# Rows of y scattered into a table in the experts' order, in a dense block followed by a routed one

## The chip, the cores and the metric

One NeuronCore of one Trainium2 chip runs the kernel. The metric is device time in microseconds (us): the median over runs of one launch. TensorE is called PE in the profile, VectorE DVE, ScalarE ACT, GpSimd POOL, and SyncE SP. SP issues most DMAs here; POOL issues the indirect ones, in which a list of 128 numbers says which rows of a table in DRAM are read or written.

## The reference

Three stages follow one another on 4608 tokens (8 batches of 576) of width 512.

```python
kv = np.einsum('bhsd,bhse->bhde', k, v)              # linear attention, 8 heads of 64
out = np.einsum('bhsd,bhde->bhse', q, kv)
x = out / np.sqrt(np.mean(out * out, -1) + 1e-6) * g_norm
h = x @ w_in                                         # dense block, 512 -> 2048 -> 512
y = (np.maximum(h, 0) + alpha * np.minimum(h, 0)) @ w_out
e_idx = np.argmax(y @ w_gate, axis=1)                # 8 experts, one for each token
gate_w = softmax(y @ w_gate)[e_idx];  eom = sigmoid(y @ w_output_gate)[e_idx]
out[mask] = gate_w * eom * (np.maximum(y[mask] @ w1[e], 0) @ w2[e])   # 512 -> 1024 -> 512
```

## The kernel before

**The dense stage** takes the tokens in 12 blocks of 384 (`NBLK`), each of three tiles of 128. For every block PE makes 16 pieces of h, then three tiles of y. The steps that follow a tile of y (`y_tail`) write it, scaled, as a pair of 16-bit floats into an SBUF tile `row` (ACT line L663, then a VectorE step), transpose it by an SP DMA into `yT` (L668) and multiply it with the gate weights (`l`, L681). `route_1` and `route_2` then find each token's expert and its place among the expert's tokens; the place, as a row number, is `pos` (L728). Beside this, small steps of the attention of later blocks run on all engines (`qs`, `rs` and `x` on POOL, `qT` transposes on SP, `ops` on PE).

**What the routing leaves in DRAM.** Two tables are written in each block. `lst` is a list of token numbers by expert, of 4 bytes an entry: POOL scatters 128 of them for each tile of a block, 36 scatters in all (L731). `ytab` holds the rows of y by token, 2052 bytes each (1024 16-bit values and one scale): SP writes them with plain DMAs (L760 and L764). `lst` is filled at the start with a number out of range (`dmy`, L1193, 8 DMAs), so that empty places of a list are skipped later.

**The expert stage** works in 38 slots of 128 tokens (and two that are skipped unless the data need them): four `s` slots of the fullest expert, run while the last dense block is still being routed, 31 `d` slots and three pairs `p` of half slots, each with one expert's weights. The `d` slots are dealt to four lanes of weights (`lane0` to `lane3`, 4 MB each, loaded by SP in 1 MB pieces when the expert of a lane changes). `tables` and `unit_tables` work out on DVE, after the last block's routing, which expert and which stretch of its list each slot has, as `tabi` and `utabi`.

For each slot the engines do this, in a written order for PE and SP: SP reads the slot's start out of `tabi` into a register and loads 128 entries of `lst` (`load_list`, L1038 and L1039); POOL gathers those rows of `ytab` into `yg` (L882); SP transposes them to `byT` (L891); PE makes `bh` (L1088) with a lane; ACT and DVE turn it into `h`; SP transposes it to `hT` (L1097); PE makes `bo` (L1110); ACT scales it; and POOL scatters it to the output by the same list (L1114). Three gather buffers (`NYG`) and five transposed ones (`NYT`) let the rows run ahead; the order in which SP issues all this is fixed when the program is built, and SP issues in order: a DMA that waits holds up those behind it.

These lines decide which gathers may be issued when (`l` counts the lists loaded, `x` the slots transposed, `t` the slots that PE has finished with, `g` the gathers):

```python
def rows_ahead():
    ...
    while done["g"] < min(done["l"], done["t"] + NYT, done["x"] + NYG, done["end"]):
        gather(done["g"])
```

Of the kernel before, what the change touches and what calls it, by code (L numbers as in the profile page):

```python
# [20 lines left out]
P = 128  # L21
# [11 lines left out]
TB = 3  # L33
# [15 lines left out]
UNITS = 2 * (len(PAIRS) + RARE)  # L49
SLOTS = FULL + len(PAIRS) + RARE  # L50
RT = 48
NLIST = E * RT * P
DUMMY = 1 << 20
ROW = DM + 1
# [10 lines left out]
def body(ctx: ExitStack, tc, q, k, v, g_norm, w_in, w_out, alpha, w_gate, w_og, w1, w2, out):  # L65
# [5 lines left out]

    ytab = dram.tile([NT, ROW], I32, name="ytab")
    lst = dram.tile([NLIST, 1], I32, name="lst")
    lsts = dram_disjoint_views(lst, TB)
    outs = dram_disjoint_views(out, SLOTS)
    ws = dram.tile([E, P, WCOLS], F16, name="ws")
# [21 lines left out]
    dve.tensor_scalar(out=base0, in0=iota_f, scalar1=float(RT * P), scalar2=None, op0=ALU.mult)  # L98
# [6 lines left out]
    for G in range(B // 2):  # L105
        for half in range(2):
            b = 2 * G + half
            pool.iota(ids[:, 9 * G + 4 * half:9 * G + 4 * half + 4], pattern=[[1, 4]], base=b * S,
                      channel_multiplier=4)
            pool.iota(ids[64 * half:64 * half + 64, 9 * G + 8:9 * G + 9], pattern=[[1, 1]],  # L110
                      base=b * S + 512, channel_multiplier=1)
    mhalf = const.tile([P, E], F32, name="mhalf")
# [63 lines left out]
    tp, yp = left("tp", 2), left("yp", 3)  # L176
    rawp, stg, cv = right("rawp", 5), right("stg", 2), right("cv", 2)
    kvp, qp, at = right("kvp", 2), right("qp", 2), right("at", 2)

    gts = [gpool.tile([P, 2, GF, BLK], F16, name=f"g{j}") for j in range(NG)]  # L180
# [471 lines left out]
    def y_tail(i, u, ps, lg, ys, rows, wait=5):  # L652
# [8 lines left out]
        rowt = yp.tile([P, ROW], I32, tag="row", name="row" + nm)  # L661
# [49 lines left out]
    def route_2(i, lg, ys, rows, oh, oh16, se):  # L711
# [23 lines left out]
        scatter(0)  # L735
        for u in range(1, TB):
            if i < NBLK - 2:
                side.extend([lambda: None] * 2 + [partial(scatter, u)])
            else:
                scatter(u)  # L740

# [11 lines left out]
        for u in range(TB):  # L753
            dve.tensor_tensor(out=rows[u][:, DM:ROW].bitcast(F32), in0=rc[:, 0, u:u + 1], in1=ys[:, u:u + 1],
                              op=ALU.mult)
            G, t = divmod(i * TB + u, 9)
            if t < 8:
                b = 2 * G + t // 4
                dst = ytab[b * S:b * S + 512, :].rearrange("(p j) c -> p j c", j=QJ)[:, t % 4, :]
                sp.dma_start(out=dst, in_=rows[u])  # L760
            else:
                for half in range(2):
                    r0 = (2 * G + half) * S + 512
                    sp.dma_start(out=ytab[r0:r0 + 64, :], in_=rows[u][64 * half:64 * half + 64, :])  # L764
# [14 lines left out]
    AHEAD, NYG, NYT = 7, 3, 5  # L779
# [4 lines left out]
    def star():  # L784
# [18 lines left out]
        dve.tensor_scalar(out=si[:, 1:2], in0=si[:, 0:1], scalar1=float(RT), scalar2=None, op0=ALU.mult)  # L803
        dve.tensor_copy(out=star_i, in_=si)
        with sp_after():
            e = sp.value_load(star_i[0:1, 0:1], min_val=0, max_val=E - 1)
            t0 = sp.value_load(star_i[0:1, 1:2], min_val=0, max_val=(E - 1) * RT)
            lv = lst.rearrange("(t p) o -> t p o", p=P)
            for j in range(STAR):
                t = bp.tile([P, 1], I32, tag="idx", name=f"idx_s{j}", bufs=10)  # L810
                i = sp.dma_start(out=t, in_=lv[bass.ds(t0 + j, 1)].rearrange("t p o -> (t p) o"))
                jobs.append(dict(nm=f"s{j}", lanes=[0], idx=t, k=kst))
            done["l"] = STAR
# [12 lines left out]
    done = dict(t=0, g=0, x=0, l=0, end=SLOTS - RARE)  # L826

    def rows_ahead():
# [3 lines left out]
        while done["g"] < min(done["l"], done["t"] + NYT, done["x"] + NYG, done["end"]):  # L832
# [27 lines left out]
    def after(x):  # L860
# [3 lines left out]
        if (layer, n) == (2, 0):  # L864
            lists(STAR + 4)
        if layer == 1 and n >= STAR - 1:
            lists(min(done["end"], n + AHEAD))
# [8 lines left out]
    def lists(end):  # L876
        while done["l"] < end:
            load_list(done["l"])
            done["l"] += 1

    def gather(n):
        pool.indirect_dma_start(out=ygs[n % NYG], out_offset=None, in_=ytab,  # L882
                                in_offset=bass.IndirectOffsetOnAxis(ap=jobs[n]["idx"][:, 0:1], axis=0),
                                bounds_check=NT - 1, oob_is_err=False)

    def turn(n):
# [7 lines left out]
        pool.tensor_tensor(out=j["msc"], in0=yg[:, DM:ROW].bitcast(F32), in1=j["k"], op=ALU.mult)  # L894
# [30 lines left out]

    def slot_k(ohs, nm):
# [6 lines left out]
    def unit_tables(es_d):  # L933
# [385 lines left out]
```

## Time and profile before

| | |
|---|---|
| median of 3 runs | 1438.72 us (1436.63 to 1442.8) |
| the profiled execution | 1453.03 us, of which 1451.3 us are its span |
| granted TensorE clock, mean of the span | 0.943 of full speed |
| PE busy | 1298.0 us, 89% of the span |
| DVE, ACT, POOL busy | 835.9, 563.2 and 327.6 us |

The profiled execution is 1.0% above the median of the timed runs. The stages lie in the span like this: the attention of the first block, the weights' conversion and the first dense block until about 320 us, the other dense blocks to about 985, the four `s` slots with the last block's routing to about 1040, then the `d` and `p` slots to 1436.9.

### The profile page before, as it was taken

To read this page: it belongs to the slowest core of one execution; us is meant where nothing else is said; L and a number is where in the kernel's file an instruction comes from. 1 tells how busy PE (TensorE), PEld (TensorE's weight loads), DVE (VectorE), ACT (ScalarE), POOL (GpSimd) and SP (SyncE) were. 2 spreads that over 40 slices of the span, in tenths; PEclk is the share of its full clock that TensorE was granted. 3 is DMA by queue.
4 is the path that set the end of the run, shared out by engine and by line. 5 is a ranking of instruction groups with operands and counts; after the bars stand their busy time and mean duration, and the time that the engine had idled before them with its cause. 6 is when DMAs were issued, how large, how long until landed. Compare 5 with 4: busy or idle time off the path is not lost. (4 is left out here: it accounts for less than half of the span.)

```text
span 1451.3 us, 22236 instructions
## 1 busy us (share of the span) xinstructions
PE 1298.0 (89%) x7586; PEld 667.3 (46%) x7586; DVE 835.9 (58%) x2470; ACT 563.2 (39%) x928; POOL 327.6 (23%) x320
## 2 busy tenths in 40 slices
PE   4679995798999989999999999999688999699996
PEld 3435542454555545555455555554233443244442
DVE  5899777568787867778696877445111211121220
ACT  3355553346555535556555655321011111011111
POOL 2023334132213332212222212011212121121211
PEclk8579997899999989999999999999899999899998
DMA  9944046757594947785846665149897888889751
GB/s 260 268 117 143 3 119 143 74 119 228 118 279 109 245 124 162 201 211 180 183 108 154 178 162 147 23 120 167 238 245 185 167 194 218 196 189 226 164 118 37
DMA packets 336628, 236.71 MB, mean 163 GB/s; under 512 B 257260, under 2 KB 290044, under 8 KB 332032
## 3 DMA queue, kind: packets, MB, share of 16 engines
q1 hardware_dynamic: 320064, 199.56, 59.4%
q0 software_dynamic: 7232, 18.92, 4.4%
q10 hardware_dynamic: 9216, 16.78, 3.5%
q8 instruction: 61, 1.00, 0.3%
q14 instruction: 55, 0.45, 0.1%
HBM read 248.07 MB, written 53.19 MB: 208 GB/s over the span
## 5 line engine op out<-in xcount | busy, mean ns | idle before, releaser
L586 PE MATMUL h<-x,wi 128*128 128x384 f16 x2304 | 419.6, 334 | 9.9 <-DMA x<-x 5.8
L605 PE MATMUL y<-wo,g 128*128 128x512 f16 x1728 | 409.7, 384 | 12.5 <-ACT g L593 7.3
L586 PEld LDWEIGHTS <-wi 128*128 128x128 f16 x2304 | 225.5, 100 | 171.8 <-issue 21.4
L605 PEld LDWEIGHTS <-g 128*128 128x128 f16 x1728 | 165.3, 98 | 198.2 <-issue 11.0
L1094 DVE CAST h_d<-br_d 128x512 f16<-128x512 f32 x62 | 26.7, 431 | 296.9 <-DMA hT_d<-h_d 187.4
L1088 PE MATMUL bh_d<-lane,byT_d 128*128 128x512 f16 x744 | 168.6, 383 | 8.4 <-DMA lane<-ws 8.4
L1110 PE MATMUL bo_d<-lane,hT_d 128*128 128x512 f16 x744 | 168.9, 384 | 7.9 <-DMA hT_d<-h_d 7.9
L593 ACT CAST g<-r 128x384 f16<-128x384 f32 x192 | 97.5, 510 | 133.0 <-DVE r L591 127.8
L591 DVE SCALAR_TENSOR_TENSOR r<-m,alphat 128x384 f32<-128x384 f32 x192 | 123.1, 642 | 24.8 <-ACT m L589 23.3
L1088 PEld LDWEIGHTS <-byT_d 128*128 128x128 f16 x744 | 73.2, 99 | 99.5 <-issue 14.6
L1110 PEld LDWEIGHTS <-hT_d 128*128 128x128 f16 x744 | 72.8, 99 | 100.1 <-DMA hT_d<-h_d 11.2
L334 POOL TENSOR_TENSOR rs<-ms,mhalf 128x8 f32<-128x8 f32 x36 | 67.6, 1879 | 225.8 <-DVE qm L337 209.7
L589 ACT ACTIVATE m<-h,scal 128x384 f32<-128x384 f32 x160 | 91.7, 575 | 39.4 <-PE h L586 36.5
L594 DVE TENSOR_TENSOR g<-r,g 128x384 f16<-128x384 f32 x160 | 93.1, 583 | 23.8 <-ACT g L593 21.4
L396 DVE SCALAR_TENSOR_TENSOR wlo_w<-rawe,es_w,whi_w 128x1024 f16<-128x1024 f32 x64 | 85.4, 1350 | 25.9 <-ACT whi_w L395 14.6
L1092 ACT ACTIVATE br_d<-bh_d 128x512 f32<-128x512 f32 x62 | 37.0, 598 | 144.9 <-PE bh_d L1088 121.1
L526 ACT ACTIVATE eab_w<-rawe 128x1024 bf16<-128x1024 f32 x64 | 67.2, 1057 | 58.7 <-DMA rawe<-in_moe_w_dram 52.2
L395 ACT ACTIVATE whi_w<-rawe,es_w 128x1024 f16<-128x1024 f32 x64 | 71.3, 1144 | 40.3 <-DMA ws<-whi_w 19.1
L1113 ACT ACTIVATE ob_d<-bo_d,msc_d 128x512 f32<-128x512 f32 x31 | 21.3, 687 | 142.3 <-PE bo_d L1110 142.3
L731 POOL DMA_INDIRECT lst<-ids,pos x36 | 37.3, 1036 | 171.9 <-DVE pos L728 109.2
L357 POOL TENSOR_TENSOR x<-xs,x 128x512 f16<-128x512 f32 x30 | 46.6, 1552 | 113.4 <-ACT x L356 84.4
L882 POOL DMA_INDIRECT yg<-ytab,idx_d x31 | 32.7, 1053 | 154.5 <-DMA idx_d<-lst 96.0
(341 smaller groups left out, 1353.9 us busy)
## 6 DMA issues: line engine op xcount, KB each, us to landing
lane<-ws SPq DMA_DIRECT2D x150, 1024.0 KB
rawe<-in_moe_w_dram SPq DMA_DIRECT2D x64, 512.0 KB
ws<-whi_w ACTq DMA_DIRECT2D x64, 256.0 KB
ws<-wlo_w SPq DMA_DIRECT2D x64, 256.0 KB
ytab<-row SPq DMA_DIRECT2D x32, 256.5 KB
q<-in_q_dram SPq DMA_DIRECT2D x16, 512.0 KB
rawwi<-in_moe_w_in_dram SPq DMA_DIRECT2D x16, 512.0 KB
rawwo<-in_moe_w_out_dram SPq DMA_DIRECT2D x16, 512.0 KB
```

The lines of the kernel that those rows point to most:

```text
L334: pool.tensor_tensor(out=rs, in0=ms, in1=mhalf, op=ALU.pow)
L395: act.activation(out=dst_h, in_=src, func=AF.Copy, scale=s)
L396: dve.scalar_tensor_tensor(out=dst_l, in0=src, scalar=s, in1=dst_h, op0=ALU.mult, op1=ALU.subtract)
L526: act.activation(out=ab.rearrange("p a b -> p (a b)"), in_=raws[4 * m + i], func=AF.Abs)
L586: pe.matmul(ps, wi[:, f // 4 * NC + c, w, fs], xt[i][:, xc, :], start=(n == 0), stop=(n == 3 * NC - 1))
L589: act.activation(out=r0, in_=ps, func=AF.Copy, scale=(scst if start else scal)[:, f:f + 1])
L591: dve.scalar_tensor_tensor(out=r, in0=r0, scalar=alphat[:, f:f + 1], in1=r0, op0=ALU.mult, op1=ALU.max)
L593: act.copy(out=hi, in_=r)
L594: (pool if start else dve).tensor_tensor(out=lo, in0=r, in1=hi, op=ALU.subtract)
L605: pe.matmul(ps, g[:, t, f % GF, us], wo[:, f, w, :], start=(start and m == 0), stop=(stop and m == 2))
L1088: pe.matmul(hp[ts], j["yT"][:, x, ts], w1_[:, w, c, hs], start=(m == 0), stop=(m == 3 * NC - 1))
L1110: pe.matmul(po[ts], hT[:, g, ts], w2_[:, w, f, :], start=(m == 0), stop=(m == 3 * NFE - 1))
```

## The change

The token lists go. In the changed kernel `ytab` has a row for every place of every expert (8 times 4608), and the row that is scattered carries the token's number: its width grows from 513 to 528 words (2112 bytes), with the scale in word 512 and the token in word 513. POOL copies the token numbers into the row tile (L758) and scatters the whole tile to `pos` (L761), so SP's plain writes of rows and POOL's scatters of lists are both replaced by one indirect DMA a tile. The row tiles are three fixed ones rather than a pool of buffers, and in blocks 0 to 9 the scatters have the whole `ytab` as their target, in blocks 10 and 11 separate views of it. A slot's row numbers follow from its table entry by arithmetic on DVE (`slot_rows`, a few operations for all `d` slots and a few for the `p` slots), so SP loads no lists; the output's row numbers come with the gathered rows (`oidx`, L890). The lines of the later functions shift: the `yT` transposes are L682, the gathers L876, `byT` L885, the lanes' loads L1059, `hT` L1094 and the output L1111.

```diff
         pos = small.tile([P, TB], I32, tag="pos", name="pos" + nm)
         dve.tensor_copy(out=pos, in_=pf)
 
-        def scatter(u):
-            pool.indirect_dma_start(out=lsts[u], out_offset=bass.IndirectOffsetOnAxis(ap=pos[:, u:u + 1], axis=0),
-                                    in_=ids[:, i * TB + u:i * TB + u + 1], in_offset=None, bounds_check=NLIST - 1,
-                                    oob_is_err=False)
...
         for u in range(TB):
-            dve.tensor_tensor(out=rows[u][:, DM:ROW].bitcast(F32), in0=rc[:, 0, u:u + 1], in1=ys[:, u:u + 1],
+            dve.tensor_tensor(out=rows[u][:, DM:DM + 1].bitcast(F32), in0=rc[:, 0, u:u + 1], in1=ys[:, u:u + 1],
                               op=ALU.mult)
...
-                sp.dma_start(out=dst, in_=rows[u])
+            pool.tensor_copy(out=rows[u][:, DM + 1:DM + 2], in_=ids[:, i * TB + u:i * TB + u + 1])
+
+        def scatter(u):
+            pool.indirect_dma_start(out=ytabs[u] if i >= NBLK - 2 else ytab, out_offset=bass.IndirectOffsetOnAxis(ap=pos[:, u:u + 1], axis=0),
+                                    in_=rows[u], in_offset=None, bounds_check=NLIST - 1, oob_is_err=False)
...
-        while done["g"] < min(done["l"], done["t"] + NYT, done["x"] + NYG, done["end"]):
+        while done["g"] < min(len(jobs), done["t"] + NYT, done["x"] + NYG, done["end"]):
...
-                                in_offset=bass.IndirectOffsetOnAxis(ap=jobs[n]["idx"][:, 0:1], axis=0),
-                                bounds_check=NT - 1, oob_is_err=False)
+                                in_offset=bass.IndirectOffsetOnAxis(ap=jobs[n]["row"], axis=0),
+                                bounds_check=NLIST - 1, oob_is_err=False)
...
+        j["idx"] = small.tile([P, 1], I32, tag="oidx", name="oidx_" + j["nm"], bufs=NYT + 3)
+        pool.tensor_tensor(out=j["idx"], in0=yg[:, DM + 1:DM + 2], in1=j["pad"], op=ALU.add)
...
+        at = slotp.tile([P, n], F32, name="at" + nm)
+        dve.tensor_scalar(out=at, in0=st, scalar1=float(w), scalar2=col, op0=ALU.mult, op1=ALU.add)
+        dve.tensor_tensor(out=lim, in0=at, in1=lim, op=ALU.is_ge)
...
-    def load_list(n):
-        if n < len(jobs):
...
-                    r = sp.value_load(tabi[0:1, 1, s:s + 1], min_val=0, max_val=NLIST // w - 1)
-                    i = sp.dma_start(out=t[x * w:(x + 1) * w], in_=lst.rearrange("(t p) o -> t p o", p=w)[bass.ds(r, 1)]
-                                     .rearrange("t p o -> (t p) o"))
...
-    dmy = small.tile([P, RT], I32, name="dmy", bufs=1)
-    pool.memset(dmy, DUMMY)
-    for e in range(E):
-        sp.dma_start(out=lst.rearrange("(e p c) o -> e p (c o)", e=E, p=P)[e], in_=dmy)
```

On POOL, around the scatters of block 0, this stands before (`lst` takes the token numbers `ids`; `x16` and `rs` belong to the attention of block 1, `qs` to that too; what an instruction waits for stands in brackets, DMASW for an indirect DMA):

```order
L357 TENSOR_TENSOR x16_0_8_2390<-xs_0_8_2371,x16_0_8_2390 128x512 [waits DMAHW4_49,DMAHW2_49,DMAHW5_49,DMAHW0_49,Activation_49]
L731 DMA lst_61<-ids_90,pos_0_2508 49152x1 [waits DMAHW7_49,DMAHW3_49,DVE_49]
L731 DMA lst_61<-ids_90,pos_0_2508 49152x1 x2
L293 TENSOR_TENSOR qs_1_2_2877<-q_1_2_2193,qsc_1_2_2870 128x512 [waits Activation_49]
L334 TENSOR_TENSOR rs_1_0_2818<-ms_1_0_2816,mhalf_107 128x8 [waits DVE_49]
```

And this in the changed kernel, at the same place:

```order
L371 TENSOR_TENSOR x16_0_8_2402<-xs_0_8_2383,x16_0_8_2402 128x512 [waits DMAHW5_49,DMAHW4_49,DMAHW7_49,DMAHW0_49,Activation_49]
L761 DMA ytab_61<-row0_194,pos_0_2519 36864x528 [waits DVE_49]
L761 DMA ytab_61<-row1_195,pos_0_2519 36864x528 [waits DMASW0_49,DVE_49]
L758 COPY row0_194<-ids_89 128x1
L761 DMA ytab_61<-row2_196,pos_0_2519 36864x528 [waits DMASW1_49,DVE_49]
L758 COPY row1_195<-ids_89 128x1
L758 COPY row2_196<-ids_89 128x1 [waits DMASW2_49]
L307 TENSOR_TENSOR qs_1_2_2885<-q_1_2_2207,qsc_1_2_2878 128x512 [waits DMAHW1_49,Activation_49]
L348 TENSOR_TENSOR rs_1_0_2827<-ms_1_0_2825,mhalf_125 128x8 [waits DVE_49]
```

The three scatters of a block waited for nothing of one another before; now each waits on POOL until the one ahead has landed, the copies of the next block's token numbers wait for the same, and `qs` and `rs` stand behind all of them.

On SP, from the last routing into the `d` slots, this is the order before (the register and list steps of `idx_d16`, `idx_d24` and `idx_d9` are like those shown, and are left out, as are the register loads of the lanes):

```order
L1097 DMA_TRANSPOSE hT1_s2_11880<-h161_s2_11877 128x8x128
...
L1039 DMA idx_d0_11912<-lst_61 128x1
...
L1039 DMA idx_d8_11923<-lst_61 128x1
...
L1062 DMA lane1_11762<-ws_62 128x4096
L1097 DMA_TRANSPOSE hT0_s3_11994<-h160_s3_11991 128x8x128
L1097 DMA_TRANSPOSE hT1_s3_12014<-h161_s3_12011 128x8x128
...
L1039 DMA idx_d1_12016<-lst_61 128x1
...
L891 DMA_TRANSPOSE byT_d0_12038<-yg1_11263 128x8x128
...
L1062 DMA lane2_11763<-ws_62 128x4096
...
L1062 DMA lane0_11261<-ws_62 128x4096
...
L891 DMA_TRANSPOSE byT_d24_12119<-yg1_11263 128x8x128
L891 DMA_TRANSPOSE byT_d1_12123<-yg2_11264 128x8x128
```

And in the changed kernel:

```order
L885 DMA_TRANSPOSE byT_d0_11874<-yg1_11241 128x8x128
L885 DMA_TRANSPOSE byT_d8_11880<-yg2_11242 128x8x128
L885 DMA_TRANSPOSE byT_d16_11886<-yg0_11240 128x8x128
L885 DMA_TRANSPOSE byT_d24_11925<-yg1_11241 128x8x128
...
L1059 DMA lane1_11742<-ws_60 128x4096
...
L1094 DMA_TRANSPOSE hT0_s3_11960<-h160_s3_11957 128x8x128
L1094 DMA_TRANSPOSE hT1_s3_11980<-h161_s3_11977 128x8x128
...
L1059 DMA lane2_11743<-ws_60 128x4096
...
L1059 DMA lane0_11239<-ws_60 128x4096
...
L885 DMA_TRANSPOSE byT_d1_12048<-yg2_11242 128x8x128
```

The list loads are gone, and four `byT` transposes stand ahead of the first pieces of `lane1` and of the `hT` transposes of `s3`, where before three of them stood behind these and the fourth behind the first pieces of `lane0`.

## Rows read from the trace of the kernel before

**Rows 1.** The page: its span, and PE's busy time

```profile
span 1451.3 us, 22236 instructions
...
PE 1298.0 (89%) x7586; PEld 667.3 (46%) x7586; DVE 835.9 (58%) x2470; ACT 563.2 (39%) x928; POOL 327.6 (23%) x320
```

**Rows 2.** Windows: dense blocks, then transition; length, busy by engine, clock, DMA share, GB/s

```profile
320.00:985.00 665.00, 640.71 (x4069) 343.71 (x4068) 488.04 (x1454) 345.06 (x557) 151.34 (x111) 0.99 0.66 165
985.00:1130.00 145.00, 119.49 (x558) 52.71 (x556) 42.08 (x162) 21.64 (x36) 27.88 (x36) 0.91 0.87 204
```

**Rows 3.** DMA issues: count, median us from issue to landing

```profile
lst<-ids,pos POOLq DMA_INDIRECT x36, 11.2
...
yg<-ytab,idx_d POOLq DMA_INDIRECT x31, 3.5
...
out_dram<-ob_d,idx_d POOLq DMA_INDIRECT x31, 4.7
...
yg<-ytab,idx_s POOLq DMA_INDIRECT x4, 7.8
```

**Rows 4.** Window behind block 0's scatters (PE, PEld, DVE, ACT, POOL, clock, DMA, GB/s)

```profile
260.00:264.00 4.00, 0.58 (x4) 0.13 (x2) 2.21 (x5) 1.83 (x4) 0.00 (x0) 1.00 2.40 27
```

**Rows 5.** Timeline there on ACT, SP and PE: start, us, instructions, idle before

```profile
252.81 0.72 ACT L663 ACTIVATE row<-g,sr 128x512 f16<-128x512 f32 x1 [2.61 <-DMA ytab<-row]
...
254.78 16.15 SPq L668 DMA_TRANSPOSE yT<-row  x3
276.48 1.23 SPq L360 DMA_TRANSPOSE x<-x  x1
...
269.27 0.40 PE L681 MATMUL l<-wg,yT 128*128 128x32 f16 x8 [8.68 <-DMA yT<-row]
...
280.48 1.79 PE L586 MATMUL h<-x,wi 128*128 128x384 f16 x10
```

**Rows 6.** Timeline behind block 1's scatters, on POOL and PE

```profile
304.34 1.07 POOL L731 DMA_INDIRECT lst<-ids,pos  x1 [0.17 <-DVE xinv L346]
...
312.43 2.04 POOL L293 TENSOR_TENSOR qs<-q,qsc 128x512 f32<-128x512 f32 x2 [2.99 <-DVE qsc L129]
...
328.32 0.84 PE L320 MATMUL ops<-kv,qT 128*128 128x128 f16 x12 [1.28 <-DMA qT<-q]
```

**Rows 7.** Timeline from the tables to the d slots, on DVE, SP, POOL

```profile
1012.35 0.20 DVE L1006 CAST tabi<-tab 128x93 int32<-128x93 f32 x1
...
1016.35 3.74 SPq L1039 DMA_DIRECT2D idx_d<-lst  x4
...
...
1022.01 10.68 SPq L1097 DMA_TRANSPOSE hT_s<-h_s  x2
...
1040.88 4.23 SPq L1062 DMA_DIRECT2D lane<-ws  x6
1045.83 11.40 SPq L891 DMA_TRANSPOSE byT_d<-yg  x2
...
1019.25 1.12 POOL L882 DMA_INDIRECT yg<-ytab,idx_d  x1 [9.36 <-DMA idx_d<-lst]
```

**Rows 8.** The same stretch on PE

```profile
1033.97 8.27 PE L1110 MATMUL bo_s<-lane,hT_s 128*128 128x512 f16 x24 [10.57 <-DMA hT_s<-h_s]
1044.75 15.88 PE L1088 MATMUL bh_d<-lane,byT_d 128*128 128x512 f16 x72 [2.50 <-DMA lane<-ws]
...
1072.06 7.78 PE L1088 MATMUL bh_d<-lane,byT_d 128*128 128x512 f16 x23 [3.29 <-DMA lane<-ws]
1079.68 5.34 PE L1110 MATMUL bo_d<-lane,hT_d 128*128 128x512 f16 x24
```

**Rows 9.** PE's waits, 1085 to 1130 us and 1205 to 1265: total, times, longest

```profile
PE bh_p L1088 <- DMA lane<-ws: 5.9, 1, 5.9
...
PE bh_p L1088 <- DMA lane<-ws: 7.0, 1, 7.0
PE bo_d L1110 <- DMA hT_d<-h_d: 7.0, 4, 4.6
```

More of the change, by code (lines that the diff above doesn't have):

```diff
@@ L49 @@
 UNITS = 2 * (len(PAIRS) + RARE)
+USIDES = [p[3] for p in PAIRS] + [(u, u + 1) for u in range(2 * len(PAIRS), UNITS, 2)]
 SLOTS = FULL + len(PAIRS) + RARE
-RT = 48
-NLIST = E * RT * P
+NLIST = E * NT
 DUMMY = 1 << 20
-ROW = DM + 1
+ROW = DM + 16
 WCOLS = 4 * NC * FE
@@ L111, in body @@
                       base=b * S + 512, channel_multiplier=1)
+    row_i = const.tile([P, 2], I32, name="row_i")
+    pool.iota(row_i[:, 0:1], pattern=[[1, 1]], base=0, channel_multiplier=1)
+    for side_ in range(2):
+        pool.iota(row_i[side_ * HALF:(side_ + 1) * HALF, 1:2], pattern=[[1, 1]], base=0, channel_multiplier=1)
+    row_f = const.tile([P, 2], F32, name="row_f")
+    dve.tensor_copy(out=row_f, in_=row_i)
+    unit_f = const.tile([P, UNITS // 2], F32, name="unit_f")
+    for x, us in enumerate(USIDES):
+        for side_, u in enumerate(us):
+            pool.memset(unit_f[side_ * HALF:(side_ + 1) * HALF, x:x + 1], float(u))
+    zero_i = const.tile([P, 1], I32, name="zero_i")
+    pool.memset(zero_i, 0)
     mhalf = const.tile([P, E], F32, name="mhalf")
@@ L175, in body @@
     wpool, xp, gpool = left("wpool", 1), left("xp", 2), left("gpool", 1)
-    tp, yp = left("tp", 2), left("yp", 3)
+    tp, yp = left("tp", 2), left("yp", 1)
     rawp, stg, cv = right("rawp", 5), right("stg", 2), right("cv", 2)
     kvp, qp, at = right("kvp", 2), right("qp", 2), right("at", 2)
+    rowts = [yp.tile([P, ROW], I32, name=f"row{u}", bufs=1) for u in range(TB)]
+    for t in rowts:
+        pool.memset(t[:, DM:ROW], 0)
     gts = [gpool.tile([P, 2, GF, BLK], F16, name=f"g{j}") for j in range(NG)]
@@ L660, in y_tail @@
                                  op1=ALU.mult)
-        rowt = yp.tile([P, ROW], I32, tag="row", name="row" + nm)
+        rowt = rowts[u]
         row = rowt[:, 0:DM].bitcast(F16)
@@ L802, in star @@
         dve.tensor_scalar(out=si[:, 0:1], in0=mx, scalar1=-1.0, scalar2=float(E), op0=ALU.mult, op1=ALU.add)
-        dve.tensor_scalar(out=si[:, 1:2], in0=si[:, 0:1], scalar1=float(RT), scalar2=None, op0=ALU.mult)
+        dve.tensor_scalar(out=si[:, 1:2], in0=si[:, 0:1], scalar1=float(NT), scalar2=row_f[:, 0:1], op0=ALU.mult,
+                          op1=ALU.add)
+        gi = small.tile([P, STAR], I32, tag="gis", name="gis", bufs=1)
+        dve.tensor_scalar(out=gi, in0=slot_f[:, 0:STAR], scalar1=float(P), scalar2=si[:, 1:2], op0=ALU.mult, op1=ALU.add)
         dve.tensor_copy(out=star_i, in_=si)
+        for j in range(STAR):
+            jobs.append(dict(nm=f"s{j}", lanes=[0], row=gi[:, j:j + 1], pad=zero_i, k=kst))
         with sp_after():
             e = sp.value_load(star_i[0:1, 0:1], min_val=0, max_val=E - 1)
[L807 to L813, printed above, removed]
             rows_ahead()
@@ L966, in unit_tables @@
         dve.tensor_copy(out=used, in_=total)
-        k = slot_k(ohs, "kunit")
-        for x, us in enumerate([p[3] for p in PAIRS] + [(u, u + 1) for u in range(2 * len(PAIRS), UNITS, 2)]):
-            for h, u in enumerate(us):
-                hs = slice(h * HALF, (h + 1) * HALF)
-                dve.tensor_copy(out=bpools["kp"][hs, x:x + 1], in_=k[hs, u:u + 1])
+        rows, pads = slot_rows(ohs, st, HALF, row_f[:, 1:2], "u")
+        for t, v in zip(bpools["units"], (slot_k(ohs, "kunit"), rows, pads)):
+            dve.tensor_copy(out=t, in_=v)
     def tables():
@@ L1006, in tables @@
         dve.tensor_copy(out=tabi, in_=tab)
+        rows, pads = slot_rows(ohs, st, P, row_f[:, 0:1], "d")
         kslot = slot_k(ohs, "kslot")
```

118 lines of the change are left out of this document (52 added, 66 removed).

## The prediction

> **What bounds the kernel now.** I began with the busy times of the page: PE works 1298.0 of 1451.3 us [rows 1], so the kernel is PE's, and only PE's idle time (153 us) or its time at the lower clock can be won; none of the edits touches PE's own work. Then I cut the span into stages. In the dense blocks from 320 to 985 us PE is idle for 24.3 us in all, in the 145 us around the transition to the experts for 25.5 [rows 2]. That sends the reader to three places, each read in the timeline: the scatters of block 0 around 250 us [rows 4, 5], the passage from the last routing to the first `d` slots [rows 7, 8], and a few waits of PE later among the slots [rows 9]. At each the reader should look at what PE waited for, and what had delayed that.
>
> **Place A, blocks 0 and 1.** The 36 list scatters move 512 bytes each and take 11.2 us to land, while the scatters of 2048-byte output rows, 512 times the data, land in 4.7 [rows 3]. What that does to others shows behind block 0: in the window from 260 to 264 us the DMA share is 2.40 (more than what all engines can be busy) at 27 GB/s, and PE works 0.58 of 4 us [rows 4]. The three `yT` transposes of block 1 need 16.15 us, and PE stands still for 8.68 us until they come, at 269.27 [rows 5]. The rest of the price is clock: PE comes back at half speed and reaches the sixth piece of h of this block at 280.48. (Such a piece is 12 matmuls.)
>
> The Trainium skill, DMA: Bandwidth & Descriptors, Specifications, says that below 512 bytes a DMA does a read-modify-write. By that the small writes are the cause, and rows of 2112 bytes would be rid of it. The trace agrees in the 11.2 against 4.7 us, though it doesn't show that the transposes' delay comes from the scatters.
>
> In the changed kernel the lists are gone and POOL scatters whole rows. Each of the first three waits for the one ahead to land, and ACT's write of the row tile of block 1 waits for the landing of the same tile of block 0. The nearest price for a landing is that of the output scatter, 4.7 us, with nearly the same bytes to scattered rows of DRAM; the gathers bound it from 3.5 to 7.8 [rows 3]. The output scatters run in a stage with a higher DMA share than the dense one (0.87 against 0.66 [rows 2]), so I take about 4.2. Starting at some 249.3 us they land at 253.5, 257.7 and 262. ACT's first row, which now waits 2.61 us for an SP write and starts at 252.81 [rows 5], starts at 253.5, about the same; the second and third at 257.7 and 262, later than today by 1 to 5 us. But a transpose should take the 1.23 us of the next one in that queue [rows 5] rather than a third of 16.15, so the first `yT` is there at about 256, the last at about 264.5, and PE has pieces of h between them rather than one gap of 8.68. I work out the sixth piece at 268 to 274 instead of 280.48: 6 to 12 us, of which later waits may eat some. I take 8, with 3 and 12 as ends.
>
> **The other blocks.** There POOL is held for two landings and three issues of about 1.07 us a block, some 11 us instead of 4. What is late next is `qs`, hence `qT`, hence `ops`. The tightest place is block 1: scatter at 304.34, `qs` at 312.43, `ops` at 328.32, which already waits 1.28 us for `qT` [rows 6]. With 4.2 us a landing the third scatter ends at 304.3 + 2 x 4.2 + 1.07 = 313.8, plus the `x` step between: `qs` is 1.5 to 2.5 us late and so is PE, once. In the later blocks PE needs what `qs` and `rs` make later behind `pos` than here, so this work covers the scatters, to a landing of some 5 us as I judge; at 7 us each block would lose a few us. The 24.3 us that PE idles in this stage [rows 2] are small waits of other kinds and stay. Term: -2, ends 0 and -10.
>
> The Trainium skill, DMA: Bandwidth & Descriptors, Anatomy of one DMA — SWDGE (gpsimd) path, fits a POOL DMA at 2.0 us plus its bytes over 436 GB/s, so 2.6 us for these 270 KB, an estimate. By it the chain would cost nothing in any block and the gain of place A would be some 3 us more; no row here is as low, and the sum uses the rows.
>
> SP loses 40 row writes and POOL gains 36 copies and 38 `oidx` additions of a single column each; DVE gains six small operations a table. POOL works 327.6 of 1451.3 us [rows 1], so this is covered, except where DVE's table is waited for (below). The eight fills of the lists at the start go too; DVE's work covers them there, and I count nothing.
>
> **Place B, into the d slots.** The table is ready at 1012.35; SP then loads four lists from 1016.35 to 1020.1, and POOL's first gather of a `d` slot, idle for 9.36 us before, begins at 1019.25 [rows 7]. Without lists it can begin when the row numbers are there: six DVE operations behind the table, of 0.20 us each as the cast of 93 columns took [rows 7], two of them over more columns, about 1.4 us: 1013.8, or earlier if DVE is itself released sooner. Against that stands SP's new order: the first pieces of `lane1` and the `hT` transposes of `s3` come behind `byT_d24`. That slot's gather needs the buffer of `d0`: gather at 1013.8, landed by 1017.5 (3.5 us [rows 3]), transposed by 1019, gather of `d24` landed by 1023.5. So `hT` of `s3` starts at 1023 to 1025.5 rather than 1022.01 [rows 7], and PE's `bo_s3` moves from 1033.97 to 1034 to 1037.5 [rows 8]. This costs 0 to 3.5 us.
>
> Behind it more is won. Today the next six lane pieces leave at 1040.88, behind two lists and three `byT`, and the two `byT` after them hold SP for 11.40 us from 1045.83 [rows 7], since their gathers started late. PE pays with waits of 2.50 us at 1044.75 and 3.29 at 1072.06 for lanes, and 23 matmuls in 7.78 us where 24 take 5.34 [rows 8], together 2.50 + 3.29 + 2.4 = 8.2. In the new order only `hT` and the lanes stand there, and `byT_d1`, gathered long before. The pieces leave about 3.5 to 7 us sooner and the last ones over 10 sooner, so all of it can go: 8.2 less 0 to 3.5, with some small waits between that go too. I take 7, ends 0 and 10.
>
> **Place C, the later slots.** Each slot saves SP one register load and one list, 3.74 / 4 = 0.93 us [rows 7], and the wait for the table's entry with it. SP is late where a lane changes: PE waits 5.9 us at `p0`, 7.0 at another `p` and 7.0 for `hT` in four waits [rows 9], 19.9 together, followed by half clock. Two or three slots' savings reach each such lane load, so I take 2 to 2.7 us at each pair and 1 at the `hT`s: 5, ends 1 and 9.
>
> **Sum.** 8 - 2 + 7 + 5 = 18 us off an execution of 1453.03, so 1435, or 0.9876 of it. The median of the runs is 1438.72, 1.0% below the profiled execution; the same share of it is 1421.
>
> **Rivals.** *Half the gain is absorbed.* At place A the clog might come from the blocks' other transfers, and DVE may then set the pace; in the slots, the lanes' 1 MB pieces may be what limits (0.87 DMA share around the transition [rows 2]), whoever issues them when. For it: the DMA share. Against: 27 GB/s at a share of 2.40 is no load by bytes [rows 4]. It gives 0 to 3 us at A, 0 at B, 2 at C, less 2 in the blocks: 1436 to 1439.
>
> *The chain of scatters holds POOL (the other side).* If a row scatter lands in 7.8 us, as the gathers beside a lane load did [rows 3], POOL is held for 2 x 7.8 + 1.07 = 16.7 us behind each `pos`. In block 1 `qs` starts at 321 or later instead of 312.43 and `ops` comes 8 us late [rows 6]; in blocks 2 to 9 some 3 us each, 24 us; place A gives nothing. That is 32 less 12 from B and C, so slower by 20: 1458, or 1450 to 1465. It decides from about 6.5 us. Against it speak the 4.7 of the output scatters and 3.5 of the gathers.
>
> *SP's new order costs.* If gather `d24` lands late (7.8 instead of 3.5 us, twice), `hT` of `s3` starts at 1031 rather than 1022.01 and PE stands for 9 us more; the 8.2 don't make up for it. That gives 8 - 2 - 1 + 5 = 10: 1429.
>
> *The whole gain.* All ends at the good side: 12 + 10 + 9 = 31: 1408.
>
> **How the numbers follow.** The forecast and its neighbours (the good ends, and SP's order at a cost) hold 0.70, half absorbed 0.18, the slow chain 0.12. The predicted time is 1421. A difference under 0.5%, 7.2 us, can't be told from no change in this kernel; the 0.18 is that case, nearly whole. The likeliest alone spans 1408 to 1431. To leave out no more than 2 in 10, the range takes in the absorbed case: 1406 to 1440; the slow chain's 0.12 and some of the best end stay outside.
>
> **What would show it.** Right: no stretch of high DMA share at a few GB/s around 260 us, `yT` of block 1 in under 8 us for three; row scatters landing in 4 to 5 us; PE at the sixth piece of h at 268 to 274; gathers of `d` slots starting by 1014 (less what was won before); no waits for lanes between `bo_s3` and the second `d` slots; `ops` of block 1 late by about 2 us. Wrong: POOL waiting for its own scatters with `rs` or `qs` on PE's path in later blocks; PE standing longer than 10.57 us ahead of `bo_s3`; or the waits for lanes as long as before, which would mean that the transfers and not SP's order set them.

## The result and the profile after

The changed kernel took 1389.73 us (median of 4 runs, 1386.57 to 1399.04) against 1440.76 for the kernel before in the same runs (1436.63 to 1447.81): a ratio of 0.9654, 95% interval 0.9625 to 0.9684. The forecast was 1421, with 1406 to 1440 as its range. The profiled execution took 1399.04 us; the first two lines of its page answer to [rows 1], the two windows to [rows 2]:

```profile
span 1396.8 us, 21921 instructions
...
PE 1279.8 (92%) x7586; PEld 664.7 (48%) x7586; DVE 838.1 (60%) x2476; ACT 560.6 (40%) x928; POOL 333.4 (24%) x410
```

```profile
320.00:985.00 665.00, 650.68 (x4149) 349.46 (x4148) 500.90 (x1547) 345.60 (x562) 156.57 (x148) 1.00 0.62 167
985.00:1130.00 145.00, 131.74 (x649) 59.52 (x648) 30.38 (x76) 23.18 (x37) 36.37 (x61) 0.95 0.93 231
```

PE works less in all (1279.8 against 1298.0 us, with the same matmuls), since less of its work falls to the lower clock (the mean granted clock of the span is 0.964 instead of 0.943), and it does more in each window. The DMA issues of after (count, median us to landing), for [rows 3]:

```profile
ytab<-row,pos POOLq DMA_INDIRECT x36, 3.0
yg<-ytab,rowd POOLq DMA_INDIRECT x31, 4.1
...
out_dram<-ob_d,oidx_d POOLq DMA_INDIRECT x31, 5.5
```

**Where the time went.** `rk` is PE's ranking step, once a block and the same in both kernels, so its times cut the program into stages. Timeline of PE before, the first `rk` of blocks 0, 1, 3, 4 and 11, and then the same of after:

```profile
247.75 0.20 PE L715 MATMUL rk<-oh,tri 128*128 128x24 f16 x1 [3.58 <-DVE oh L707]
...
301.74 0.18 PE L715 MATMUL rk<-oh,tri 128*128 128x24 f16 x1
...
451.27 0.18 PE L715 MATMUL rk<-oh,tri 128*128 128x24 f16 x1
...
539.48 0.18 PE L715 MATMUL rk<-oh,tri 128*128 128x24 f16 x1
...
996.53 0.19 PE L715 MATMUL rk<-oh,tri 128*128 128x24 f16 x1 [0.74 <-DVE oh L707]
```

```profile
247.39 0.20 PE L729 MATMUL rk<-oh,tri 128*128 128x24 f16 x1 [3.76 <-DVE oh L721]
...
289.79 0.18 PE L729 MATMUL rk<-oh,tri 128*128 128x24 f16 x1
...
442.87 0.18 PE L729 MATMUL rk<-oh,tri 128*128 128x24 f16 x1
...
517.45 0.18 PE L729 MATMUL rk<-oh,tri 128*128 128x24 f16 x1
...
969.75 0.19 PE L729 MATMUL rk<-oh,tri 128*128 128x24 f16 x1 [0.74 <-DVE oh L721]
```

From block 0 to block 1: 53.99 us before, 42.40 after, so place A gave 11.6. From block 1 to block 11: 694.79 and 679.96, so the other blocks gave 14.8, of which 13.6 lie between blocks 3 and 4 alone (88.21 and 74.58). The `bo` slot that began at 1079.68 before [rows 8] begins at 1042.63: counted from `rk` of block 11 that is 83.15 and 72.88, so place B gave 10.3. PE ends at 1436.9 and 1381.8, so 357.2 and 339.2 us follow: place C gave 18.0. Together 54.7, against 54.5 us between the spans (the first `rk` comes 0.4 us sooner, and 0.5 us more follow PE's end).

Read in the same way, the second profiles of the two kernels (before_again and after_again below) give 12.4 for place A, 15.5 for the other blocks, 7.7 for place B and 23.6 for place C. So how the 28 to 31 us of B and C divide between the two is known only to some 3 to 6 us.

Not all of the 13.6 us is waiting. Windows from `rk` of block 3 to that of block 4, before and after:

```profile
451.27:539.48 88.21, 80.17 (x506) 42.50 (x504) 64.37 (x189) 43.49 (x69) 24.43 (x13) 0.94 0.70 172
```

```profile
442.87:517.45 74.58, 73.24 (x479) 40.01 (x478) 62.24 (x183) 42.94 (x68) 18.07 (x16) 1.00 0.71 195
```

PE has 27 matmuls fewer in this stretch of the changed kernel; they stand in the stretches ahead of it. From block 2 to block 3 the changed kernel takes 4.0 us longer (79.22 before, 83.17 after), and blocks 1 to 4 together gave 10.1.

**Place A**, the window of [rows 4] and the timeline of [rows 5] in the changed kernel, on ACT, SP and PE:

```profile
260.00:264.00 4.00, 1.64 (x18) 1.07 (x18) 1.29 (x3) 1.68 (x3) 1.18 (x2) 1.00 0.48 39
```

```profile
252.46 0.72 ACT L677 ACTIVATE row<-g,sr 128x512 f16<-128x512 f32 x1 [2.71 <-DMA ytab<-row,pos]
...
256.20 0.72 ACT L677 ACTIVATE row<-g,sr 128x512 f16<-128x512 f32 x1 [1.17 <-DMA ytab<-row,pos]
...
261.96 0.72 ACT L677 ACTIVATE row<-g,sr 128x512 f16<-128x512 f32 x1 [3.17 <-DMA ytab<-row,pos]
...
254.04 10.98 SPq L682 DMA_TRANSPOSE yT<-row  x3
...
267.90 2.11 PE L600 MATMUL h<-x,wi 128*128 128x384 f16 x12
```

The DMA share is 0.48 instead of 2.40. The rows now wait for the scatters' landings, which is what the 10.98 us of the three transposes hold, and the piece of h that began at 280.48 begins at 267.90.

**Place B** on SP and PE, for [rows 7, 8]:

```profile
987.50 9.72 SPq L885 DMA_TRANSPOSE byT_d<-yg  x4
998.99 1.14 SPq L1059 DMA_DIRECT2D lane<-ws  x2
1000.23 8.46 SPq L1094 DMA_TRANSPOSE hT_s<-h_s  x2
...
1009.88 7.01 PE L1107 MATMUL bo_s<-lane,hT_s 128*128 128x512 f16 x24 [13.26 <-DMA hT_s<-h_s]
1016.73 3.62 PE L1085 MATMUL bh_d<-lane,byT_d 128*128 128x512 f16 x16
```

The wait ahead of `bo_s3` grew from 10.57 to 13.26 us, but in this profile none follows it until the second pair. All of PE's waits from 975 us on (total, times, longest), against [rows 9]:

```profile
PE bo_s L1107 <- DMA hT_s<-h_s: 13.3, 1, 13.3
PE bh_p L1085 <- DMA lane<-ws: 8.0, 1, 8.0
```

### The profile page after: what moved, and what is told of

Same layout as the page of the kernel before. It is cut to its first block, busy times and chain, and to the rows that moved or that the text cites. A ratio compares the mean times of both kernels' runs of the same rounds, so it can differ in the third digit from the quotient of the medians.

```text
span 1396.8 us, 21921 instructions
## 1 busy us (share of the span) xinstructions
PE 1279.8 (92%) x7586; PEld 664.7 (48%) x7586; DVE 838.1 (60%) x2476; ACT 560.6 (40%) x928; POOL 333.4 (24%) x410
## 5 line engine op out<-in xcount | busy, mean ns | idle before, releaser
L600 PE MATMUL h<-x,wi 128*128 128x384 f16 x2304 | 408.7, 328 | 9.6 <-ACT m L603 5.1
L600 PEld LDWEIGHTS <-wi 128*128 128x128 f16 x2304 | 221.8, 98 | 164.7 <-issue 12.1
L1107 PE MATMUL bo_d<-lane,hT_d 128*128 128x512 f16 x744 | 165.5, 379 | 0.1
L1085 PE MATMUL bh_d<-lane,byT_d 128*128 128x512 f16 x744 | 165.3, 379 | 0.0
L761 POOL DMA_INDIRECT ytab<-row,pos x36 | 37.3, 1037 | 215.1 <-DVE pos L742 110.7
L1111 POOL DMA_INDIRECT out_dram<-ob_d,oidx_d x31 | 31.8, 1026 | 188.6 <-ACT ob_d L1110 187.7
L371 POOL TENSOR_TENSOR x<-xs,x 128x512 f16<-128x512 f32 x30 | 37.0, 1234 | 104.8 <-ACT x L370 79.2
```

Of the source, the lines that this page charges most:

```text
L600: pe.matmul(ps, wi[:, f // 4 * NC + c, w, fs], xt[i][:, xc, :], start=(n == 0), stop=(n == 3 * NC - 1))
L1085: pe.matmul(hp[ts], j["yT"][:, x, ts], w1_[:, w, c, hs], start=(m == 0), stop=(m == 3 * NC - 1))
L1107: pe.matmul(po[ts], hT[:, g, ts], w2_[:, w, f, :], start=(m == 0), stop=(m == 3 * NFE - 1))
```

## Experiments

The ratios are to the kernel before in the same job, with 95% intervals. "Dense" is the time on PE from the first `rk` of block 0 to that of block 11 in the one profile of each, "slots" from there to PE's end.

| kernel | median us | ratio | dense | slots |
|---|---|---|---|---|
| before, and again | 1440.76, 1444.47 | | 748.8, 748.2 | 440.4, 434.4 |
| after | 1389.73 | 0.9654 (0.9625 to 0.9684) | 722.4 | 412.1 |
| after_again, after_ref | 1386.51, 1392.74 | -, 0.9669 (0.9642 to 0.9695) | 720.3, 718.2 | 403.1, 401.4 |
| lists4 | 1452.52 | 1.0039 (0.9998 to 1.0079) | 783.7 | 405.5 |
| lists512 | 1394.39 | 0.9627 (0.9559 to 0.9695) | 719.8 | 409.6 |
| plainwrites | 1404.83 | 0.9701 (0.9647 to 0.9756) | 728.6 | 411.8 |
| w4 | 1393.50 | 0.9628 (0.9578 to 0.9677) | 731.6 | 408.0 |
| w64 | 1390.32 | 0.9627 (0.9558 to 0.9696) | 727.9 | 405.8 |
| w512 | 1393.53 | 0.9658 (0.9591 to 0.9724) | 731.1 | 402.3 |
| w4adj | 1608.66 | 1.1131 (1.1091 to 1.1171) | 925.8 | 423.8 |
| w4s64 | 1393.32 | 0.9635 (0.9607 to 0.9663) | 729.1 | 409.2 |
| listchain | 1410.87 | 0.9751 (0.9698 to 0.9804) | 721.6 | 425.6 |
| listloads | 1411.49 | 0.9742 (0.9690 to 0.9794) | 721.3 | 432.2 |
| loads_reg | 1403.69 | 0.9704 (0.9656 to 0.9751) | 717.2 | 418.3 |
| loads_dma | 1402.12 | 0.9708 (0.9679 to 0.9737) | 721.5 | 414.8 |
| loads512 | 1407.84 | 0.9773 (0.9737 to 0.9809) | 717.8 | 425.7 |
| hTfirst | 1389.35 | 0.9569 (0.9520 to 0.9619) | 717.1 | 411.7 |
| hTfirst2 | 1385.75 | 0.9614 (0.9578 to 0.9650) | 717.2 | 402.3 |

The slots of one unchanged kernel differ by 11 us between profiles (401.4 to 412.1), so single profiles tell only more than that. The kernels ran in different jobs, in which the median of the kernel before was 1440.76 to 1446.87, so medians of two jobs compare only to some 6 us; the ratios are each within one job.

**Both kernels again.** No edit.

> The kernel before, unchanged, for a second profile. In the first one a POOL step of the attention (x, 128x512) took 9.07 us in the dense blocks where its kind takes 1.15, SP's transpose of its result and the weight loads behind it came late, and PE lost 5.45 us in one wait and more at the lower clock: between the routing of block 3 and that of block 4 88.2 us passed, against 74.6 in the changed kernel. Theory 1 (a chance of that execution): the step takes 1.2 to 2 us here and the stretch 74 to 78 us. Rival (it belongs to the order of work of the kernel before): 9 us and 86 to 90 us again.

> The changed kernel, unchanged, for a second profile. Both theories of the step that took 9.07 us: here none over 2 us, and 74 to 76 us from the routing of block 3 to that of block 4. PE's wait for hT of s3 ahead of bo_s3 (13.26 us) and the one lane wait at the second pair (7.95 us) return within 1 us.

The long POOL step came back in the kernel before and not in the changed one. Timeline of POOL in the first profile of before, in its second, and in after (`x` of the same tile):

```profile
502.43 9.07 POOL L357 TENSOR_TENSOR x<-xs,x 128x512 f16<-128x512 f32 x1 [6.91 <-ACT x L356]
```

```profile
498.35 9.07 POOL L357 TENSOR_TENSOR x<-xs,x 128x512 f16<-128x512 f32 x1 [6.89 <-ACT x L356]
```

```profile
486.63 1.56 POOL L371 TENSOR_TENSOR x<-xs,x 128x512 f16<-128x512 f32 x1 [4.09 <-ACT x L370]
```

So it is no chance, and blocks 3 to 4 took 87.8 us again (76.9 in after_again). Of the two waits that were expected to return in after_again, the 13.26 us ahead of `bo_s3` did (13.3); the 7.95 us for a lane at the second pair did not (0.6 is all that `bh_p` waits for lanes there), so that one does not belong to every execution. How PE comes to wait can be read in the first profile of before, a window and the timeline behind it (SP, ACT, PE):

```profile
505.00:510.00 5.00, 5.00 (x29) 2.70 (x28) 5.00 (x11) 2.79 (x5) 5.00 (x1) 1.00 0.18 66
```

```profile
511.52 1.71 SPq L360 DMA_TRANSPOSE x<-x  x1
...
519.20 1.06 ACT L526 ACTIVATE eab_w<-rawe 128x1024 bf16<-128x1024 f32 x1 [10.42 <-DMA rawe<-in_moe_w_dram]
...
520.71 2.32 PE L605 MATMUL y<-wo,g 128*128 128x512 f16 x5 [5.45 <-ACT g L593]
```

SP's transpose of the step's result, and with it the weight loads queued behind, leave only at its end, 511.50; ACT waits 10.42 us for such a load, PE 5.45 for ACT. DVE is busy without a break beside the step (5.00 of 5 us), but so it is beside the short step of after. What the two have in common is their end: each ends within 0.03 us of a small DVE step that takes 1.1 us where its kind takes 0.17 and 0.23. The two DVE steps, in before and in after:

```profile
510.41 1.11 DVE L127 TENSOR_SCALAR kvi<-pw_ekv 128x8 int32<-128x8 int32 x1
```

```profile
487.09 1.12 DVE L703 TENSOR_SCALAR ls<-ys,kt 128x3 f32<-128x3 f32 x1
```

It looks as if the two engines took turns, and POOL's came late in before; that is inferred. The Trainium skill, GPSIMD Engine Reference, Specifications, says that POOL shares its SBUF interfaces with DVE and contends with DVE instructions in a 2-port mode or with two SBUF inputs; the trace agrees in that most of DVE's time beside the step goes to such steps of two inputs (`wlo_w`, `r`, `g`), though three small ones of a single input lie between them and no run isolates it.

**The list scatters, put back beside the row scatters.** lists4 adds to the changed kernel (with half as many places an expert):

```diff
+            pool.indirect_dma_start(out=lsts[u], out_offset=bass.IndirectOffsetOnAxis(ap=pos[:, u:u + 1], axis=0),
+                                    in_=ids[:, i * TB + u:i * TB + u + 1], in_offset=None, bounds_check=NLIST - 1,
+                                    oob_is_err=False)
```

> The changed kernel with the list scatters of before beside its row scatters: 36 of 128 token numbers, 4 bytes each, into a table that nobody reads (the tables hold half as many places an expert, which is room enough). Theory 1 (these small scatters clog the DMA engines): they land in 9 to 12 us, the three yT transposes of block 1 again need over 10 us, the routing of block 1 comes 50 to 54 us behind that of block 0 instead of 42.4, and the whole is 10 to 20 us slower than the changed kernel: 1400 to 1412. Rival (SP's plain row writes held up ACT and the transposes): 42 to 45 us there, and 1388 to 1395 in all.

It lost the whole gain, some 53 to 63 us and not the 10 to 20 expected, all in the dense part. The lists landed in 7.3 us (median) and the row scatters in 5.7 instead of 3.0. Between the first two blocks it took 48.1 us, so place A came back only in part. In the dense part the kernel before is only 26.4 us slower than the changed one, lists4 61.3, so the loss is more than the lists cost before. In lists4 the rows stand behind the lists on POOL, and POOL's waits for the landing of rows grow from 43.4 us in after to 88.1. lists512 has rows of 128 constants as its source and token numbers, ready from the start, as its index:

> As lists4, but each of the 36 extra scatters writes 128 rows of 512 bytes, of constants, to the rows of a table by token. Theory 1 with size as the cause: they land in 3 to 4 us, 42 to 45 us from the routing of block 0 to that of block 1, and 1388 to 1396 in all, though 128 times the bytes move. Rival (any extra indirect scatter costs this much, by its 128 descriptors or by POOL's time): over 9 us to land and as slow as lists4.

It lost 5 us at most, but its scatters went out in the first 105 us of the kernel, so that it did not tell size from place. plainwrites adds SP's row writes of before:

> The changed kernel with SP's plain writes of the rows of before beside its scatters: 40 DMAs of 128 or 256 KB into a table by token that nobody reads. Theory 1 (the small list scatters were the cause of the delay behind block 0): the writes cost 0 to 4 us, the routing of block 1 stays 42 to 46 us behind that of block 0. Rival (SP's row writes were): 50 us or more there, and 8 to 15 us slower in all than 1389.7.

42.4 us between the first two blocks became 40.5 (40.4 in after_again and after_ref): the row writes had no part in place A. In all they cost some 12 to 15 us by the medians and 5 to 7 by the ratios, spread out, more than expected, in a schedule that differs from after's in many rows.

**What about the lists costs.** The three kernels w4, w64 and w512 have the same order of work. They add, with `n` words a write (1, 16, 128):

```diff
+        dve.tensor_scalar(out=pf, in0=pf, scalar1=0.0, scalar2=row_f[:, 0:1], op0=ALU.mult, op1=ALU.add)
+        dve.tensor_scalar(out=pk, in0=pf, scalar1=float(128 // n), scalar2=None, op0=ALU.mult)
...
+            pool.indirect_dma_start(out=lsts[u], out_offset=bass.IndirectOffsetOnAxis(ap=pk[:, u:u + 1], axis=0),
+                                    in_=ident[:, 0:n].bitcast(I32), in_offset=None, bounds_check=..., oob_is_err=False)
```

> The changed kernel with three extra scatters a block, ready with pos like its own: 128 writes of 4 bytes each, 512 bytes apart, into small tables that nobody reads; w64 and w512 are the same but for the bytes of a write, with the same order of work on every engine. (In lists512 the extra scatters waited for nothing and went out early in the kernel, so it did not tell size from place.) Theory 1 (writes of a few bytes clog the DMA engines): over 7 us to land, own row scatters 5 to 6 us instead of 3.0, the routing of block 11 comes 740 to 785 us behind that of block 0 instead of 720 to 722, and 1410 to 1450 us in all. Rival (it is the number of scatters and POOL's time for them): w4, w64 and w512 agree within 5 us.

> As w4 with 64 bytes a write. Theory 1 with the size as such: between w4 and w512. Theory 1 with a threshold above 64 bytes: as w4, within 6 us.

> As w4 with 512 bytes a write, 128 times its bytes. Theory 1: 3 to 4 us to land, own row scatters under 3.5 us, 718 to 730 us from the routing of block 0 to that of block 11, and 1388 to 1400 us in all. Rival: as slow as w4.

All three are within 3.2 us of each other and 3.8 of after: theory 1, that the size of a write is the cause, fell. The extra scatters are not free, though. The dense part of the three is 6 to 13 us longer than that of the changed kernel, and their totals hide it: in their profiles 7.8 us follow PE's end where 15.0 do in after, for a reason that no run shows. What lists4 has and w4 has not is that words of one expert lie side by side. w4adj and w4s64 change only the factor in `pk`, from 128 to 1 and to 16:

> As w4, but the 128 words of an extra scatter lie side by side (4 bytes apart, 512 bytes in all), as the token numbers of one expert do in the lists of before. Only the addresses differ from w4. Theory 4 (it is not the size of a write but that writes of several DMA engines fall into the same few lines of DRAM): row scatters behind it land in over 5 us instead of 3, the dense blocks take 745 to 790 us from the routing of block 0 to that of block 11 (728 to 732 in w4, w64 and w512), and 1410 to 1455 us in all. Rival (the lists of lists4 cost by their place in the schedule, the views or something else): as w4, 1390 to 1397.

> As w4, with the words 64 bytes apart. Theory 4 with lines of 64 bytes: as w4. With lines of 512 bytes or more: between w4 and w4adj, or as w4adj.

Against w4, adjacent words cost 215 us more (theory 4 expected 20 to 60), words 64 bytes apart nothing. In w4adj, behind block 0, the row scatter behind the three extra ones takes 24 us to land (POOL's timeline: the next waits 22.86). A transpose that SP issues at 256.11 keeps PE waiting until 278.88 (PE's timeline, third line). In between nothing works and next to no transfer moves (window: all engines 0.00, DMA share 0.00; the DMA share is 0.00 in every window of 4 us from 264 to 280):

```profile
257.19 1.36 POOL L765 DMA_INDIRECT ytab<-row,pos  x1 [0.30 <-issue]
281.61 0.99 POOL L765 DMA_INDIRECT ytab<-row,pos  x1 [22.86 <-DMA ytab<-row,pos]
...
278.88 0.40 PE L696 MATMUL l<-wg,yT 128*128 128x32 f16 x8 [18.44 <-DMA yT<-row]
```

```profile
264.00:268.00 4.00, 0.00 (x0) 0.00 (x0) 0.00 (x0) 0.00 (x0) 0.00 (x0) 0.67 0.00 0
```

In w4s64 the same two rows are 3.4 us apart:

```profile
253.20 1.36 POOL L765 DMA_INDIRECT ytab<-row,pos  x1 [0.30 <-issue]
256.60 0.99 POOL L765 DMA_INDIRECT ytab<-row,pos  x1 [1.84 <-DMA ytab<-row,pos]
```

These kernels show something else too: w4, w64, w512 and w4s64 have the long step of POOL again (9.15, 9.15, 9.15 and 8.94 us) and 82.6 to 84.9 us between blocks 3 and 4, without any adjacent words. So adjacent words are not needed for it. But it goes with the small scatters behind `pos`: both profiles of before, lists4, w4adj (8.94 us each in these two) and the four above have it, and none of the kernels without such scatters does (the step takes 5.63 us in plainwrites and less than 3 in the others). The change takes these scatters out of POOL's order; by what steps this shortens the POOL step, no run shows.

**The lists of the slots.** listchain puts them back as waits: SP reads a register and loads 128 zeros for each `d` and `p` slot, and POOL adds them to the row numbers. listloads drops the addition; loads_reg has only the first of these two lines, loads_dma only the second, with a fixed address:

```diff
+                    r = sp.value_load(tabi[x * HALF:x * HALF + 1, 0, j["at"][0]:j["at"][0] + 1], min_val=0, max_val=E - 1)
+                    i = sp.dma_start(out=t[x * w:(x + 1) * w], in_=zl.rearrange("(e p) o -> e p o", p=P)[bass.ds(r, 1)]
```

> The changed kernel with the lists of before put back into the d and p slots as a chain of waits only: for each slot SP loads a register and 128 zeros of a table in DRAM, as many slots ahead as before, and POOL adds them to the row numbers before the gather. Theory 1 (the gain among the slots is that gathers no longer wait for lists that stand behind other waiting work on SP): 20 to 28 us of the 28 behind the last routing go again: 1410 to 1418. Rival (it is SP's own time for the loads): as in listloads.

> As listchain, but nobody waits for the zeros: the gathers use the row numbers directly. Theory 1: SP's own time costs 2 to 7 us: 1392 to 1397. Rival (SP's time is what the lists cost): 20 to 28 us, as listchain.

> As listloads, with the register load of each slot but no list DMA. Theory 2 (SP is in series with the lanes and transposes it issues, and a register load costs it about 1 us with its wait): 1398 to 1406, so half of the 21 us of listloads or more. Rival (the lists' DMAs of 4 bytes a partition cost it, by their size or by waits for earlier DMAs): 1388 to 1395.

> As listloads, with the list DMA of each slot from a fixed address and no register load. Theory 2 (the register loads are the larger part): 1391 to 1400. Rival (the DMA is): 1402 to 1412.

Against the changed kernel (1389.7 to 1392.7) the chain costs 18 to 21 us, loads that nobody waits for 19 to 22, the register loads 11 to 14 and the DMAs 9 to 12. By the ratios (0.9654 and 0.9669 for the changed kernel) it is 12 to 14, 10 to 13, 5 to 7 and 6 to 8: in the same order, and a third to a half smaller. So theory 1, that gathers waited for lists, fell, and SP's own time is the cost, about half by each. SP's waits for DVE's `h` say why (us in total, times, longest), in before from 1030 to 1425 us, in listloads and in after from 1000 to 1370:

```profile
SPq L1097 <- DVE h_d L1095: 10.4, 7, 2.7
```

```profile
SPq L1120 <- DVE h_d L1118: 20.8, 13, 4.3
```

```profile
SPq L1094 <- DVE h_d L1092: 38.0, 26, 3.9
```

An SP that waits for `h` is on time. In the changed kernel it is so at 26 transposes (there are two for each of the 31 `d` slots), before at 7 (27 and 8 in the second profiles): for most slots SP came late before.

> As loads_dma, but 512 bytes a partition instead of 4 (into one buffer, so that each load also waits until the one before has landed). If small pieces cost here as in the scatters: 5 us or more faster than loads_dma. If it is SP's issue and its place in the queue: within 4 us of loads_dma.

1407.84 against 1402.12: larger pieces are no faster, but the single buffer is a wait of its own, so this says nothing clear of the size.

**The new wait ahead of bo_s3.** In hTfirst the condition for gathers and `byT` is

```diff
-        if layer == 1 or n < STAR:
+        if layer == 1 or 0 < n < STAR:
             rows_ahead()
```

and hTfirst2 also moves the first pieces of `lane1` (the first entry of `FIRST` from `(2, 0, 1, 0)` to `(1, 3, 1, 0)`).

> The changed kernel with one pass of gathers and byT transposes of the d slots left to a later point of SP's written order, so that the hT transposes of s3 stand ahead of byT_d0 to byT_d24, as before the change, but behind the first pieces of lane1. Theory 1 (the order costs PE the wait of 13.26 us ahead of bo_s3): the wait shrinks to 3 to 8 us and 5 to 9 us are won: 1381 to 1385. Rival (the transposes of s3 are held by the lane's 2 MB, wherever the byT stand): the wait stays over 10 us and the time within 3 us of 1389.7.

> As hTfirst, with the first two pieces of lane1 also behind the hT transposes of s3. In hTfirst the wait ahead of bo_s3 was still 10.09 us, since the transposes stood behind these 2 MB. Theory 3 (transposes wait for the transfers issued ahead of them): the wait falls below 5 us and the kernel gains 5 to 9 us on the changed one in the same job. Rival (what is won there is lost to later waits for lanes, which come later): the wait falls, and the time stays within 3 us.

> The changed kernel again, as the reference for hTfirst2, loads_dma and loads512 on the same chip: 1386 to 1393.

In hTfirst the wait was still 10.09 us, as the rival had it, so the `byT` cause some 3 us of it and the lane's pieces ahead the rest; the median is that of after, though the ratio, 0.9569, is the lowest of all, so a small gain is open here too. In hTfirst2 it is gone, and these are PE's waits from 965 us on:

```profile
PE bh_d L1085 <- DMA lane<-ws: 6.0, 3, 2.7
PE bh_p L1085 <- DMA lane<-ws: 5.1, 2, 3.5
PE bo_d L1107 <- DMA hT_d<-h_d: 0.8, 2, 0.6
```

11.9 us, against 13.2 in the profile of after_ref: what the transposes won, lanes that load later took. Its median is the lowest of all here, 7 us below after_ref, but the intervals overlap and the slots of the two profiles agree within 1 us; whether it is faster is not settled.

## Why the prediction was wrong

The direction and the three places were right; the sum was 18 us where the profile gave 54.5 and the medians 51.

- **Place A: 8 forecast, ends 3 and 12; 11.6 measured.** The chain was read rightly. ACT's three rows began at 252.46, 256.20 and 261.96 us, against 253.5, 257.7 and 262 in the forecast, though the three transposes took 10.98 us with their waits and not under 8. The piece of h (the seventh of its block; the prediction counts it as the sixth) began at 267.90, at the early end of 268 to 274. The 8 left room for what later waits would eat, and they ate next to nothing. The median landing of the row scatters, 3.0 us, is nearer to the 2.6 us that the prediction estimated by the Trainium skill, DMA: Bandwidth & Descriptors, Anatomy of one DMA — SWDGE (gpsimd) path, than to the output scatter's 4.7; but at place A the rows waited about as long as 4.2 us a landing had it, so the 3 us more that this estimate promised did not come from there. The cause that the prediction took from the Trainium skill, DMA: Bandwidth & Descriptors, Specifications, writes below 512 bytes, is not what the runs show: size alone does nothing (4, 64 and 512 bytes cost the same), and adjacent words cost 215 us in w4adj. That adjacent words are the cause in the kernel before itself is carried over from lists4 and w4adj; the kernel before was not run with its lists spread out.
- **The other blocks: -2 forecast, +14.8 measured.** "Small waits of other kinds and stay" is the step that failed. One of them, PE waiting for ACT's `g`, with the time at the lower clock behind it, was the end of a chain that starts at the 9.07 us step of POOL; the prediction took PE's idle time as one sum and did not follow this wait back. The chain is worth some 8 to 10 us, as the four kernels w4 to w4s64 show, which have the step and 82.6 to 84.9 us in the stretch where after has 74.6; the rest of the 13.6 is work that stands in other blocks. The step went with the list scatters (above); why, stays open. The cost that was forecast did come, and in its size, but one block later than said. In block 1 `qs` came 9.3 us behind its first scatter instead of 8.1, and `ops` waited 1.23 us instead of 1.28. In block 2, where `ops` had no wait before, POOL's `qs` stands behind the landings and `ops` waits 2.42 us for `qT`:

```profile
374.09 0.18 POOL L758 COPY row<-ids 128x1 int32<-128x1 int32 x1 [1.64 <-DMA ytab<-row,pos]
...
388.92 1.46 PE L334 MATMUL ops<-kv,qT 128*128 128x128 f16 x12 [2.42 <-DMA qT<-q]
```

- **Place B: 7 forecast, ends 0 and 10; 10.3 measured (7.7 in the second profiles).** Step by step as written: `bo_s3` came 2.7 us later, counted from `rk` of block 11 (13.26 us of wait instead of 10.57; 0 to 3.5 forecast), and the waits behind it went.
- **Place C: 5 forecast, ends 1 and 9; 18.0 measured (23.6 in the second profiles).** The mis-sized term. "SP is late where a lane changes" was wrong: SP was late at most slots, so the time it saves adds up from slot to slot instead of two or three at a time. The price of a list, 0.93 us, was right in size: over 34 lists it makes 32 us, of which 10 to 22 reach the end, by the ratios and the medians of listloads.
- **The rivals.** None came: no median landing near 6.5 us, no absorbed half. The range left out the case in which more than the listed waits goes, which is what happened.

## What to carry to other kernels

Before pricing a transfer, look at where its neighbours land: three indirect DMAs, each of 128 words side by side, stopped all other transfers for some 16 us, and the same words 64 bytes apart did not. An engine that only issues transfers can still be the one in series: count how often it waits for the work it passes on, since one that rarely waits is late, and then time taken from it reaches the end. And follow each wait of the bounding engine back to its start even in a stage where the sum of waits is small, since a change can move the order laid by a scheduler, and with it these waits, in ways that the diff does not name.

## What the runs showed of the hardware

- Three indirect writes, each of 128 words of 4 bytes to 512 adjacent bytes of DRAM, held up a row scatter behind them, which took about 24 us to land, and a transpose of SP beside it; with the words 64 bytes apart the same row scatter was followed by the next after 3.4 us, as with 512 bytes apart (w4). Between 4 and 64 bytes no distance was tried.
- A POOL step that takes 1.56 us in after took 9.07 us beside DVE work in both profiles of the kernel before, and 8.94 to 9.15 us in the six kernels that have small scatters behind `pos` beside the rows (lists4, w4, w64, w512, w4adj, w4s64). Both the long and the short step end as a small DVE step that takes 1.1 us instead of 0.2 ends.
